# The written-out opening of a spectral mixer with a gated feed-forward: a new order, sixteen of its operations on GpSimd, and a root of its own for each of the first two blocks

## The chip, the core and the metric

The kernel runs on one core of a Trainium2 chip. The metric is device microseconds of one execution. The engines are named as the profile names them: PE is TensorE, whose weight loads stand apart as PEld; DVE is VectorE; ACT is ScalarE; POOL is GpSimd; SP is SyncE, which here only issues DMAs.

## The reference, cut to what matters

The input x is 1 x 2048 x 448 in fp32. It is normalised over its rows of 448, and the sum of three things is returned: x itself, a two-dimensional Fourier filter of the normalised x, and a gated feed-forward layer of it with 1792 inner columns.

```python
xn = layernorm(x)                                  # over the last axis, eps 1e-5
A = irfft2(rfft2(xn) * (w_r + 1j * w_i))           # 2048 x 448
gate, up = xn @ W_gate, xn @ W_up                  # 448 -> 1792
B = (gate * (gate > 0) * up) @ W_down              # 1792 -> 448
return x + A + B
```

## The kernel before

**Tiling.** The 2048 rows are 16 blocks of 128, number n2 = q + 4j, in four chunks q taken in the order 0, 2, 1, 3. The 1792 inner columns are 14 slabs f of 128, in groups of 5, 5 and 4. An fp32 operand is split into an fp16 upper part and an fp16 remainder, and a product is three fp16 passes. For slab f and chunk q, PE does 20 passes of 512 columns over gate (g = 0) and up (g = 1) into two PSUM banks (`gu_full`, L757) and a few "half" passes (`gu_half`, L764). ACT and DVE turn the banks into h (L799, L803, L807, L811), and `dn_mm` (L834) multiplies h by W_down. The Fourier part is cut into many DVE operations that run beside the feed-forward.

**What a block needs before PE can use it.** Statistics on DVE (`st`, L255 and L258), a reciprocal root on ACT (`sq`, L266) with three or four small corrections on DVE (`rs`, L271 to L275), the normalised fp32 block (`xn` on DVE at L297, or `ax` on ACT at L295), its upper half (`hi` or `hx`, ACT, L304 and L306), two small copies on POOL (`cp`, L310 and L311), and the remainder (`lo`, DVE, L321 and L322). For chunk 0, PE transposes the block (`tpA`, `tpB`, L337) and it is copied from PSUM into T (`vev` on DVE). The blocks of chunk 2 are transposed by DMA (`dm`, L330).

**What a weight needs.** A load (`lw`), the sum of its squares on ACT (`wsq`, L185), a sum over all partitions on POOL (`par`, `partition_all_reduce`, L188), two small scale operations on DVE (`wsc`, L191 and L195), its upper part on ACT (`whi`, L699) and its remainder on DVE (`wlo`, L703). For W_down the same steps are `lwd`, `wdq`, `wdp` (the all-reduce over `wdm`, L188), `wdsc` (ten small DVE operations), `wdh` (ACT, L731) and `wdl`.

**What sets the order.** In the opening, about the first 45 us, every engine's queue is in the order of a hand-written string of names, `OPENING`; each name issues one piece. Behind it, a scheduler puts units (`gu`, `dn`) and Fourier pieces into order. All queues are in order: an instruction that waits holds all that stand behind it on its engine. `keep_warm(n)` issues n matmuls on zeros (L1094), 21 of them at the start and 4 after the first transposes (`kw4`). Slab 0 is done in halves of 256 columns (`hh`, `lh`, `hl`), slab 1 too (`ah`, `bh`, `ch`), since two blocks of chunk 0 are ready before the other two.

**POOL before.** In the opening it does the memsets at the start, the small copies and the all-reduces, and nothing else.

Of the kernel before, what the change touches and what calls it, by code (L numbers as in the profile page):

```python
# [29 lines left out]
OPENING = """lx0 st0 lx4 st4 sqA rsA ax4 hi0 lx8 st8 lx12 xn0 lw cp0 lw lw lw hx4 warm tpA4 st12 tpA0 lo0 lx6 sqB rsB cp4 lo4  # L30
wsqW0g0 tpB0 kw4 tpB4 wsqW0g1 lx2 hi8 parW0g0 wscW0g0 lwd1 whiW0g0 vevA0 parW0g1 wscW0g1 vevA4 hh00 tpA8 whiW0g1
ly4 hi12 lw hh10 lw lw lw wsqW1g1 wsqW1g0 vevB4 vevB0 hl00 wloW0g0 parW1 wloW0g1 tpA12 vevA12 hl10 vevA8 lh00
cp8 xn8 lh10 hh11 lw ax12 lh11 wscW1 whiW1g0 hh01 cp12 whiW1g1 lh01 lw lo8 wsqW2g1 wsqW2g0 tpB8 ah00 lwd0 lo12
tpB12 wsqW3g0 vevB8 wloW1g0 ah10 wsqW3g1 vevB12 ah01 parW2 ah11 lwd2 wloW1g1 wscW2 bh00 hl11 hl01 lx14 whiW2g0
bh01 hp0 ch10 whiW2g1 lw st2 bh11 st6 re0 wloW2g0 bh10 wsqW4g1 ch00 ch11 tm0 gu2g0 parW3 wscW3 st14 wsqW4g0
whiW3g0 wloW2g1 ch01 ly0 parW4 wscW4 whiW3g1 wloW3g1 lw wsqW5g1 lx10 whiW4g0 wloW3g0 gh0 re1 st10 gu2g1 tm1 hp2
sqC rsC wsqW5g0 xn6 gu3g0 re2 parW5 wscW5 whiW5g0 tm2 wloW4g0 xn10 xn14 hx14 lwd4 hx6 lo6 hi10 whiW5g1 lo10
gu4g0 hx2 wloW5g0 whiW4g1 cp14 xn2 wdq0 gl0 cp10 gu3g1 wloW4g1 lo14 lwd3 wdq4 wdq2 cp2 re3 tm3 cp6 wloW5g1 gh1
gu4g1 gh2 wdq3 ly12 lo2 hp4 wdq1 wdp wdsc wdh4 dm10 gl1 re4 ly8 wdh3 gl2 gu5g1 tm4 gh4 dm14 gl4 dm6 gu5g0 dm2
re5 lfd gz0g0 wdl3 gz0g1 tm5 hp6 gh3 gl3 rz0 gh5 wdl4 gl5 wdh1 wdl1 wdh2 wdl2 n0 wdh0 wdl0 gz1g0 tz0 gz1g1 rz1  # L40
hz0 tz1 hz1 lz0 lz1
"""
EXPMASK = 0x7F800000
EXPONE = float(1 << 23)
# [100 lines left out]
def tile_gfnet_reglu(ctx: ExitStack, tc: tile.TileContext, x, xr, xi, wgu, wd, wf, c_fd, c_fm, c_im, c_row, c_id,  # L145
                     out):
    nc = tc.nc
    V, A, P, G = nc.vector, nc.scalar, nc.tensor, nc.gpsimd
# [28 lines left out]
    eps = mt([128, 1], F32, "eps")  # L177
# [23 lines left out]
    def ft(shape, dt, name, bufs=1):  # L201
        return fwd_pool.tile(shape, dt, name=name, bufs=bufs)
# [4 lines left out]
    warm = row_t.rearrange("p a b c -> p (a b c)")  # L207


    xr_t, xr_b = {}, {}  # L210
# [16 lines left out]
    wst, wdst, fm_t, im_t, wf_t = {}, {}, {}, {}, {}  # L227
# [22 lines left out]
    mv = {}  # L250

    def ln_stats(q, j):
        n2 = q + 4 * j
        st = ft([128, 6], F32, "bst", 2)
        V.bn_stats(st, xr_t[n2])  # L255
        if j == 0:
            mv[q] = ft([128, 4, 2], F32, "mv", 2)
        V.bn_aggr(mv[q][:, j, :], st)  # L258

    rst = {}  # L260

    def ln_sd(q, js=(0, 1, 2, 3)):
        w = ft([128, 4, 4], F32, "rs", 3)
        n = len(js)
        rst[q, js[0]] = w[:, :, 0:n], mv[q][:, js[0]:js[-1] + 1, :]
        A.activation(w[:, 0, 0:n], rst[q, js[0]][1][:, :, 1], AF.Abs_reciprocal_sqrt, bias=eps)  # L266

    def ln_rstd(q, js=(0, 1, 2, 3), bias=False):
        w, m = rst[q, js[0]]
        r0, t, r, nm = (w[:, i] for i in range(4))  # L270
        V.scalar_tensor_tensor(t, m[:, :, 1], 1e-5, r0, op0=OP.add, op1=OP.mult)  # L271
        V.scalar_tensor_tensor(t, t, -0.5 * 2048, r0, op0=OP.mult, op1=OP.mult)
        V.scalar_tensor_tensor(r, t, 1.5 * 2048, r0, op0=OP.add, op1=OP.mult)
        if bias:
            V.scalar_tensor_tensor(nm, m[:, :, 0], -1.0, r, op0=OP.mult, op1=OP.mult)  # L275
        for i, j in enumerate(js):
            rst[q, j] = r[:, i:i + 1], nm[:, i:i + 1], m[:, i, 0:1]

    xn, tt, xn_b = {}, {}, {}
    tts = [ft([128, 8, 128], F16, f"tt{i}") for i in range(4)]  # L280
# [6 lines left out]
        tt[n2] = tts[state.setdefault("tn", 0) % 4]  # L287
        state["tn"] += 1

    def ln_xn(n2, act=False):  # L290
        xn_b[n2] = free.pop(0)
        xn[n2] = xn_b[n2].rearrange("p g c k -> p (g c k)")[:, 0:D]
        r, nm, mean = rst[n2 % 4, n2 // 4]
        if act:
            A.activation(xn[n2], xr_t[n2], AF.Identity, scale=r, bias=nm)  # L295
        else:
            V.tensor_scalar(xn[n2], xr_t[n2], mean, r, op0=OP.subtract, op1=OP.mult)  # L297

    def ln_hi(n2, fused=False):
        new_tt(n2)  # L300
        o = tt[n2].rearrange("p a b -> p (a b)")[:, 0:D]
        r, nm, _ = rst[n2 % 4, n2 // 4]
        if fused:
            A.activation(o, xr_t[n2], AF.Identity, scale=r, bias=nm)  # L304
        else:
            A.activation(o, xn[n2], AF.Copy)  # L306
# [9 lines left out]
        ln_copy(n2)  # L316
        free.append(xr_b.pop(n2))

    def ln_lo(n2):
        x, t = xn[n2], tt[n2].rearrange("p a b -> p (a b)")  # L320
        V.tensor_tensor(t[:, 512:896], x[:, 0:384], t[:, 0:384], op=OP.subtract)  # L321
        V.tensor_tensor(t[:, 448:512], x[:, 384:448], t[:, 384:448], op=OP.subtract)  # L322
        free.append(xn_b.pop(n2))

    tp, last = {}, {}
# [350 lines left out]
    wt, wdt, wsc = {}, {}, {}  # L676
# [17 lines left out]
        for i, k in enumerate(gs):  # L694
            wsc[f, k] = sc[:, i:i + 1]

    def w_hi(f, g):
        w = wt[f, g] = mt([128, 8, 128], F16, "wt", 2 * NR + 4)
        A.activation(w[:, 0:4, :], wst[f, g], AF.Copy, scale=wsc[f, g])  # L699

    def w_lo(f, g):
        st, sc, w = wst[f, g], wsc.pop((f, g)), wt[f, g]
# [386 lines left out]
    seq1 = [(r + 4 * k, r) for k in (0, 1) for r in range(3)]  # L1089
    seq2 = [(r, r + 4) for r in range(3)] + [(3, 3)]  # L1090

    def keep_warm(n):
        for _ in range(n):
            P.matmul(wps, warm[:, 0:128], warm, start=True, stop=True)  # L1094

    pieces = {"lfd": lambda: nc.sync.dma_start(fd_t, c_fd),
              "lw": load_wn, "warm": lambda: keep_warm(NWARM),
              **{f"kw{n}": (lambda n=n: keep_warm(n)) for n in (1, 3, 4)},
              "wdp": lambda: wd_sum(len(groups[0])),
              "wdsc": lambda: wd_scale(0, groups[0])}  # L1100

    def piece(name, fn, *a):
        pieces[name] = lambda: fn(*a)

    for c, q in enumerate(CHUNKS[:2]):
        for js, tag in (((0, 1), "A"), ((2, 3), "B")) if c == 0 else (((0, 1, 2, 3), "C"),):
# [101 lines left out]
    for i, u in list(enumerate(units))[START + 1:-4]:  # L1208
        is_gu = u[0] == "gu"
        if is_gu:  # L1210
            _, g, f, q = u
# [4 lines left out]
        else:  # L1216
            _, g, n2, _ = u
# [69 lines left out]
```

## Time and profile before

| | us |
|---|---|
| median of 3 runs | 443.17 (442.64 to 443.61) |
| span of the profiled execution | 440.9 |
| PE busy | 435.7 (99% of the span) |
| DVE busy | 382.3 (87%) |
| ACT busy | 184.5 (42%) |
| POOL busy | 29.4 (7%) |

The span runs from the first to the last instruction of one profiled execution; the median of the runs is 2.27 us above it, which is what lies around the span. A row of the timeline gives the start, the time taken, the engine, the line, the operation, what it writes and reads, how many were merged, and in brackets the idle time before and what ended it. PEld shows when PE had to wait for weights: PE's own rows have modelled ends and hide small waits.

### The profile page before, as it was taken

The numbers are of one execution on the slowest core, as the hardware profiler recorded it, in microseconds if no ns is written. First come the engines' busy times: TensorE is split into PE (matmuls) and PEld (weight loads), VectorE is DVE, ScalarE is ACT, GpSimd is POOL, SyncE is SP. The second block draws the span as 40 slices with busy tenths as digits, with TensorE's granted clock in tenths as the row PEclk, the third lists the DMA queues.
The fourth block names the chain that finished last, engine by engine and source line by source line (L and its number), as shares of the span: only waits on it lengthen the run. The fifth ranks groups of instructions, "written<-read, shape, count | busy, mean of one in ns | idle before, by whom it ended". The sixth has DMA issues, their size and how long they took to land.

```text
span 440.9 us, 7429 instructions
## 1 busy us (share of the span) xinstructions
PE 435.7 (99%) x2641; PEld 221.9 (50%) x2641; DVE 382.3 (87%) x957; ACT 184.5 (42%) x396; POOL 29.4 (7%) x75
## 2 busy tenths in 40 slices
PE   8999999999999999999999999999999999999996
PEld 3744464554445545444545444444545555555664
DVE  6998496989887879999999999988997989798644
ACT  6995427392457236144023467233113332243220
POOL 3230002011100040000000020000000000000000
PEclk9999999999999999999999999999999999999999
DMA  7929895304111123332220210001111121210212
GB/s 256 301 91 198 269 364 172 70 2 107 59 49 50 47 76 119 94 118 84 86 84 1 84 43 1 0 1 42 44 43 49 54 91 34 72 55 33 89 51 104
DMA packets 37613, 39.55 MB, mean 90 GB/s; under 512 B 16535, under 2 KB 33353, under 8 KB 37577
## 3 DMA queue, kind: packets, MB, share of 16 engines
q1 hardware_dynamic: 37576, 39.09, 29.1%
q8 instruction: 20, 0.33, 0.3%
q14 instruction: 17, 0.13, 0.1%
HBM read 24.38 MB, written 3.67 MB: 64 GB/s over the span
## 4 chain that ended last, share of the span: by engine, by line
PE 90%; DVE 4%; ACT 3%; DMA 1%; issue 1%; SPq 0%; POOL 0%; ACTq 0%
PE bank L757 49%; PE bank L834 27%; PE bank L764 3%; PE fx L648 2%; PE fx L369 2%; PE fx L667 2%; PE fx L406 2%; PE bank L853 2%; ACT wt L699 1%; DMA T<-tt 1%; ACT junk L185 1%; DVE bst L255 1%; DVE wt L703 1%; DMA y<-in_xr 1%; ACT tt L304 1%
## 5 line engine op out<-in xcount | busy, mean ns | idle before, releaser
L757 PE MATMUL bank<-T,wt 128*128 128x512 f16 (+1 forms) x1160 | 252.7, 372 | 0.6 <-DVE T L345 0.5
L757 PEld LDWEIGHTS <-wt 128*128 128x128 f16 x1160 | 110.9, 98 | 127.6 <-issue 7.2
L834 PE MATMUL bank<-wdt,h 128*128 128x448 f16 x624 | 122.4, 352 | 0.0
L834 PEld LDWEIGHTS <-h 128*128 128x128 f16 x624 | 60.5, 98 | 55.1
L799 ACT ACTIVATE g<-bank 128x512 f32<-128x512 f32 x56 | 33.0, 591 | 80.4 <-PE bank L757 45.2
L807 ACT ACTIVATE h<-g 128x512 f16<-128x512 f32 x56 | 35.0, 627 | 70.1 <-DVE g L803 70.0
L803 DVE SCALAR_TENSOR_TENSOR g<-bank,g 128x512 f32<-128x512 f32 x56 | 38.2, 683 | 11.9 <-PE bank L757 6.8
L811 DVE TENSOR_TENSOR h<-g,h 128x512 f16<-128x512 f32 x56 | 38.1, 684 | 6.7 <-ACT h L807 6.4
L840 DVE SCALAR_TENSOR_TENSOR xy<-bank,dsc,xy 128x448 f32<-128x448 f32 x44 | 29.8, 676 | 5.5 <-PE bank L834 5.2
L632 ACT ACTIVATE vt<-y,fsc 128x456 f16<-128x456 f32 x15 | 10.1, 674 | 34.5 <-issue 14.0
L699 ACT ACTIVATE wt<-wst,wsc 128x512 f16<-128x512 f32 x28 | 19.3, 713 | 11.1 <-DVE wsc L195 10.3
L703 DVE SCALAR_TENSOR_TENSOR wt<-wst,wsc,wt 128x512 f16<-128x512 f32 x28 | 20.4, 742 | 0.5 <-ACT wt L699 0.3
L672 DVE SCALAR_TENSOR_TENSOR xy<-fx,fsc,xy 128x448 f32<-128x448 f32 x16 | 10.8, 680 | 10.9 <-PE fx L667 10.9
L188 POOL PARTITION_ALL_REDUCE wm<-wm x15 | 10.5, 697 | 139.9 <-ACT junk L185 136.4
L185 ACT ACTIVATE junk<-wst 128x512 bf16<-128x512 f32 x28 | 17.2, 616 | 0.0
L397 ACT ACTIVATE Xh<-X 128x456 f16<-128x456 f32 x16 | 9.3, 579 | 16.4 <-DVE X L395 9.3
L764 PE MATMUL bank<-T,wt 64*128 64x512 f16 x112 | 15.6, 380 | 0.0
L400 DVE TENSOR_TENSOR Xh<-X,Xh 128x456 f16<-128x456 f32 x16 | 9.8, 624 | 4.9 <-ACT Xh L397 4.9
L648 PE MATMUL fx<-im,vt 128*128 128x128 f16 x192 | 13.3, 219 | 0.0
L667 PEld LDWEIGHTS <-pgh 114*128 114x128 f16 x192 | 10.9, 98 | 3.8 <-issue 0.8
L648 PEld LDWEIGHTS <-vt 128*128 128x128 f16 x192 | 11.6, 98 | 1.3
L406 PE MATMUL fx<-Xh,fm 128*128 128x456 f16 x48 | 12.2, 356 | 0.0
(168 smaller groups left out, 480.1 us busy)
## 6 DMA issues: line engine op xcount, KB each, us to landing
wst<-in_wgu SPq DMA_DIRECT2D x28, 256.0 KB
sw<-y SPq DMA_DIRECT2D x56, 112.2 KB
wf<-in_wf SPq DMA_DIRECT2D x16, 228.0 KB
xy<-in_x SPq DMA_DIRECT2D x16, 224.0 KB
y<-in_xr SPq DMA_DIRECT2D x15, 224.0 KB
out<-xy SPq DMA_DIRECT2D x15, 224.0 KB
wdst<-in_wd SPq DMA_DIRECT2D x14, 224.0 KB
fm<-in_c_fm SPq DMA_DIRECT2D x4, 256.0 KB
```

The source lines that it names most:

```text
L185: A.activation(mt([128, 512], BF16, "junk", 2)[:, 0:src.shape[-1]], src, AF.Square, scale=SQ, accum_out=acc)
L648: P.matmul(o, v[:, h, w], m[:, c, :], start=(i == 0), stop=(i == 2), skip_group_check=True)
L699: A.activation(w[:, 0:4, :], wst[f, g], AF.Copy, scale=wsc[f, g])
L703: V.scalar_tensor_tensor(w[:, 4:8, :], st, sc, w[:, 0:4, :], op0=OP.mult, op1=OP.subtract)
L757: last["P"] = P.matmul(hps[f, q][g][:, cs], wt[f, g][:, a, :], Tq[q][:, b, cs], start=(start and i == 0), stop=(stop and i == len(seq) - 1 ...
L764: m = P.matmul(hps[f, q][g][:, 0:512], wt[f, g][rows, 7, :], Tq[q][rows, b, :], start=start, stop=stop).ins
L799: last["A"] = A.activation(g1s[f, q], hps[f, q][0], AF.Relu, scale=2.0 ** -22).ins
L803: last["V"] = V.scalar_tensor_tensor(g1, hps[f, q][1], 2.0 ** -22, g1, op0=OP.mult, op1=OP.mult).ins
L807: A.activation(ht[f, q][:, 0, :], g1s[f, q], AF.Copy)
L811: V.tensor_tensor(h[:, 1, :], g1s.pop((f, q)), h[:, 0, :], op=OP.subtract)
L834: last["P"] = P.matmul(ps[:, 0:D], ht[f, q][:, a, js], wdt[f][:, b, :], start=(i == 0), stop=(i == n - 1)).ins
L840: last["V"] = V.scalar_tensor_tensor(xy[:, n2, :], dps[n2][:, 0:D], dsc[:, g:g + 1], xy[:, n2, :], op0=OP.mult, op1=OP.add).ins
```

## The change

`OPENING` is replaced by another string of the same work. What differs beyond the order:

- Sixteen pieces go to POOL. Four `px` (blocks 4, 14, 6 and 10) and four `ph` (8, 6, 10, 2) are a `tensor_scalar` over 448 columns, the normalised block or its upper half straight from x. Four `pl` (4, 8, 14, 2) are the two `tensor_tensor` of the remainder. Four `pw` (W0g1, W2g0, W2g1, W4g0) are a `tensor_scalar` over 512 columns, the upper part of a weight.
- Blocks 4 and 0 each get their own root (`sq4 rs4`, `sq0 rs0`), where before one root served both (`sqA rsA`). Block 4 is loaded ahead of block 0.
- Blocks 0 and 4 are multiplied with slab 0 in quarters of 128 columns (`hq`, `lq`, `kq`); the other two blocks stay one half of 256.
- 14 warm matmuls stand at the start in place of 21; five of the eight copies from PSUM into T go from DVE to ACT (`aev`).

The scheduler's part behind the opening comes out in another order on every engine, with the same operations.

```diff
-NWARM = 21
-OPENING = """lx0 st0 lx4 st4 sqA rsA ax4 hi0 lx8 st8 lx12 xn0 lw cp0 lw lw lw hx4 warm tpA4 st12 tpA0 lo0 ...
+OPENING = """lx4 lx0 lw st4 sq4 st0 rs4 wsqW0g0 parW0g0 lw lx8 sq0 rs0 px4 lx12 warm14 wscW0g0 wsqW0g1 xn0 hx4 st8 tpA4 parW0g1 pl4
+hx0 cp0 st12 cp4 whiW0g0 wscW0g1 lw lo0 wloW0g0 lw tpA0 kw4 sqB vevA4 tpB0 aevA0 hq00 tpB4 ...
-    def ln_xn(n2, act=False):
+    def ln_xn(n2, act=False, pool=False):
...
-            V.tensor_scalar(xn[n2], xr_t[n2], mean, r, op0=OP.subtract, op1=OP.mult)
+            (G if pool else V).tensor_scalar(xn[n2], xr_t[n2], mean, r, op0=OP.subtract, op1=OP.mult)
-    def ln_hi(n2, fused=False):
+    def ln_hi(n2, fused=False, eng=None):
...
+        if eng is not None:
+            eng.tensor_scalar(o, xr_t[n2], mean, r, op0=OP.subtract, op1=OP.mult)
-    def ln_lo(n2):
+    def ln_lo(n2, eng=V):
...
-        V.tensor_tensor(t[:, 512:896], x[:, 0:384], t[:, 0:384], op=OP.subtract)
-        V.tensor_tensor(t[:, 448:512], x[:, 384:448], t[:, 384:448], op=OP.subtract)
+        eng.tensor_tensor(t[:, 512:896], x[:, 0:384], t[:, 0:384], op=OP.subtract)
+        eng.tensor_tensor(t[:, 448:512], x[:, 384:448], t[:, 384:448], op=OP.subtract)
-    def w_hi(f, g):
+    def w_hi(f, g, eng=None):
...
+            eng.tensor_scalar(w[:, 0:4, :], wst[f, g], wsc[f, g], None, op0=OP.mult)
...
+            piece(f"sq{n2}", ln_sd, q, (j,))
+            piece(f"rs{n2}", ln_rstd, q, (j,))
+            piece(f"nm{n2}", ln_bias, q, (j,))
+                                ("px", ln_xn, False, True), ("ph", ln_hi, False, G), ("pl", ln_lo, G), ("vh", ln_hi, False, V), ("dm", ln_dma),
+            piece(f"pwW{f}g{g}", w_hi, f, g, G)
```

POOL's queue at the start of the opening, before. `wm` is the buffer of the weights' sums, `tt` a transposed-to-be block, `Tl` a buffer that is cleared. An `ISA` row with names is an all-reduce; the one without names is added by the build, and it is the only one of its kind behind the start of the program.

```order
L284 MEMSET Tl_98 32x512
L310 COPY tt_100<-tt_100 128x48
L311 COPY tt_100<-tt_100 128x64
L310 COPY tt_101<-tt_101 128x48
L311 COPY tt_101<-tt_101 128x64
L188 ISA
L188 ISA wm<-wm 128x1 x2
L188 ISA wm<-wm 128x2
```

The same place now (`y_68` is the normalised block 4, `g_122` its input, `wt` a weight's two parts):

```order
L287 MEMSET Tl_98 32x512
L187 ISA
L187 ISA wm<-wm 128x1
L300 ISA
L300 TENSOR_SCALAR y_68<-g_122,mv,rs 128x448
L187 ISA
L187 ISA wm<-wm 128x1
L326 ISA
L326 TENSOR_TENSOR tt_100<-y_68,tt_100 128x384
L327 TENSOR_TENSOR tt_100<-y_68,tt_100 128x64
L315 COPY tt_101<-tt_101 128x48
L316 COPY tt_101<-tt_101 128x64
```

The nameless row stands wherever the queue goes from an all-reduce to a `TENSOR_SCALAR` or `TENSOR_TENSOR` or back, and never between an all-reduce and a `COPY`. There was one in the whole kernel; there are 13 now, all in the opening, the last of them ahead of the all-reduce over `wdm`.

POOL's queue at the end of the opening, before: the last small copies of the opening, then the all-reduce of W_down's sums.

```order
L310 COPY tt_103<-tt_103 128x48
L311 COPY tt_103<-tt_103 128x64
L310 COPY tt_101<-tt_101 128x48
L311 COPY tt_101<-tt_101 128x64
L188 ISA wdm<-wdm 128x5
```

And now, behind the twelfth nameless row:

```order
L307 ISA
L307 TENSOR_SCALAR tt_102<-y_75,mv,rs 128x448
L707 TENSOR_SCALAR wt<-wst,wsc 128x512
L307 TENSOR_SCALAR tt_103<-y_72,mv,rs 128x448
L326 TENSOR_TENSOR tt_103<-y_79,tt_103 128x384
...
L300 TENSOR_SCALAR y_80<-y_75,mv,rs 128x448
L326 TENSOR_TENSOR tt_101<-y_77,tt_101 128x384
L327 TENSOR_TENSOR tt_101<-y_77,tt_101 128x64
L315 COPY tt_102<-tt_102 128x48
L316 COPY tt_102<-tt_102 128x64
L187 ISA
L187 ISA wdm<-wdm 128x5
```

The upper part of W4g0 (the `wt` row) and the all-reduce over `wdm` moved behind all of POOL's new work; ahead of `dn_mm`, PE needs both.

ACT's queue at the start, before (`rs` is a root, `junk,wm` a sum of squares, `tt<-y` an upper half):

```order
L266 ACTIVATE rs<-mv,eps 128x2
L295 ACTIVATE y_67<-g_127,rs 128x448
L304 ACTIVATE tt_100<-y_66,rs 128x448
L306 ACTIVATE tt_101<-y_67 128x448
L266 ACTIVATE rs<-mv,eps 128x2
L185 ACTIVATE junk,wm<-wst 128x512 x2
```

And now:

```order
L265 ACTIVATE rs<-mv,eps 128x1
L184 ACTIVATE junk,wm<-wst 128x512
L265 ACTIVATE rs<-mv,eps 128x1
L184 ACTIVATE junk,wm<-wst 128x512
L311 ACTIVATE tt_100<-y_68 128x448
L311 ACTIVATE tt_101<-y_70 128x448
L705 ACTIVATE wt<-wst,wsc 128x512
```

ACT no longer makes the normalised block 4 itself; its upper half `tt_100<-y_68` now waits for POOL, and the other upper half and the first weight stand behind that wait.

More of the change, by code (lines that the diff above doesn't have):

```diff
@@ L25 @@
 LAG, AHEAD, RAMP = 1, 5, 8
-NWARM = 21
 N2ORD = [0, 8, 4, 12, 2, 10, 6, 14, 1, 9, 5, 13, 3, 11, 7, 15]
 CHUNKS = [0, 2, 1, 3]
[L30 to L38, printed above, removed]
@@ L42 @@
+gh1 gu3g0 wloW4g0 ph2 tm2 wloW5g1 pl2 wloW5g0 cp2 lo6 gu3g1 cp6 wloW4g1 gu4g0 px10 wdq2 re3 tm3 gu4g1 ly12 gh2 gl2
+lo10 pl14 hp4 cp10 wdq4 dm2 gu5g1 wdq1 gh3 wdp gu5g0 dm10 ly0 wdsc wdh4 cp14 dm6 wdh0 gl1 re4 re5 tm4 gl3 tm5 wdh3
+wdh1 dm14 gz0g0 gh4 wdl4 gl4 ly8 gh5 wdl1 gz0g1 hp6 rz0 gz1g0 gl5 tz0 gz1g1 hz0 rz1 wdl0 wdh2 wdl3 lz0 tz1 hz1 wdl2
+lz1
 """
@@ L255, in ln_stats @@
         V.bn_stats(st, xr_t[n2])
-        if j == 0:
+        if q not in mv:
             mv[q] = ft([128, 4, 2], F32, "mv", 2)
         V.bn_aggr(mv[q][:, j, :], st)
-    rst = {}
+    rst, rsb = {}, {}
     def ln_sd(q, js=(0, 1, 2, 3)):
-        w = ft([128, 4, 4], F32, "rs", 3)
+        w = ft([128, 4, 4], F32, "rs", 4)
         n = len(js)
-        rst[q, js[0]] = w[:, :, 0:n], mv[q][:, js[0]:js[-1] + 1, :]
-        A.activation(w[:, 0, 0:n], rst[q, js[0]][1][:, :, 1], AF.Abs_reciprocal_sqrt, bias=eps)
+        rsb[q, js[0]] = w[:, :, 0:n], mv[q][:, js[0]:js[-1] + 1, :]
+        A.activation(w[:, 0, 0:n], rsb[q, js[0]][1][:, :, 1], AF.Abs_reciprocal_sqrt, bias=eps)
     def ln_rstd(q, js=(0, 1, 2, 3), bias=False):
-        w, m = rst[q, js[0]]
+        w, m = rsb[q, js[0]]
         r0, t, r, nm = (w[:, i] for i in range(4))
@@ L274, in ln_rstd, with ln_bias @@
         if bias:
-            V.scalar_tensor_tensor(nm, m[:, :, 0], -1.0, r, op0=OP.mult, op1=OP.mult)
+            ln_bias(q, js)
         for i, j in enumerate(js):
             rst[q, j] = r[:, i:i + 1], nm[:, i:i + 1], m[:, i, 0:1]
+    def ln_bias(q, js):
+        w, m = rsb[q, js[0]]
+        V.scalar_tensor_tensor(w[:, 3], m[:, :, 0], -1.0, w[:, 2], op0=OP.mult, op1=OP.mult)
     xn, tt, xn_b = {}, {}, {}
@@ L695, in w_scale @@
             wsc[f, k] = sc[:, i:i + 1]
-    def w_hi(f, g):
+    def w_hi(f, g, eng=None):
         w = wt[f, g] = mt([128, 8, 128], F16, "wt", 2 * NR + 4)
-        A.activation(w[:, 0:4, :], wst[f, g], AF.Copy, scale=wsc[f, g])
+        if eng is None:
+            A.activation(w[:, 0:4, :], wst[f, g], AF.Copy, scale=wsc[f, g])
+        else:
+            eng.tensor_scalar(w[:, 0:4, :], wst[f, g], wsc[f, g], None, op0=OP.mult)
     def w_lo(f, g):
@@ L1096, in tile_gfnet_reglu @@
     pieces = {"lfd": lambda: nc.sync.dma_start(fd_t, c_fd),
-              "lw": load_wn, "warm": lambda: keep_warm(NWARM),
-              **{f"kw{n}": (lambda n=n: keep_warm(n)) for n in (1, 3, 4)},
+              "lw": load_wn, **{f"{t}{n}": (lambda n=n: keep_warm(n)) for t in ("kw", "warm") for n in range(1, 25)},
               "wdp": lambda: wd_sum(len(groups[0])),
@@ L1151, in tile_gfnet_reglu @@
             piece(f"whiW{f}g{g}", w_hi, f, g)
+            piece(f"pwW{f}g{g}", w_hi, f, g, G)
+            piece(f"vwW{f}g{g}", w_hi, f, g, V)
             piece(f"wloW{f}g{g}", w_lo, f, g)
@@ L1154, in tile_gfnet_reglu @@
             if f == 0:
+                for j in range(2):
+                    for tag, sq in (("hq", seq1[0:3]), ("lq", seq1[3:6]), ("kq", seq2)):
+                        piece(f"{tag}{g}{j}", gu_full, f, q, (g,), slice(128 * j, 128 * j + 128), tag == "hq" and j == 0,
+                              False, sq)
                 piece(f"parW{f}g{g}", w_sum, f, (g,))
```

16 lines of the change are left out of this document (10 added, 6 removed).

## The prediction

> **What bounds the kernel now.** I read the page's busy times first, then PE's timeline, then the waits of its weight loads, then POOL's timeline. The columns of a timeline row are start, time taken, engine, line, operation and, in brackets, the idle time before it and what ended it.
>
> ```profile
> PE 435.7 (99%) x2641; PEld 221.9 (50%) x2641; DVE 382.3 (87%) x957; ACT 184.5 (42%) x396; POOL 29.4 (7%) x75
> 1.22 7.46 PE L1094 MATMUL bank<-row_t 128*128 128x512 f16 x21 [1.22 <-DVE row_t L1166]
> 8.52 0.78 PE L337 MATMUL fx<-g,tt 128*128 128x128 f16 x11
> 9.13 1.03 PE L1094 MATMUL bank<-row_t 128*128 128x512 f16 x4
> 10.93 0.49 PE L757 MATMUL bank<-T,wt 128*128 128x256 f16 x3 [0.49 <-DVE T L345]
> 35.73 9.09 PE L757 MATMUL bank<-T,wt 128*128 128x512 f16 x40
> 33.09 1.63 PEld L757 LDWEIGHTS <-wt 128*128 128x128 f16 x9 [0.32 <-DVE wt L703]
> 35.19 0.12 PEld L764 LDWEIGHTS <-wt 64*128 64x128 f16 x4 [0.47 <-DVE wt L703]
> 40.33 0.76 PEld L757 LDWEIGHTS <-wt 128*128 128x128 f16 x5 [0.60 <-DMA T<-tt]
> ```
>
> PE bounds the kernel, and its work is the same before and after. Time can only be won where PE does nothing useful: before 8.52 (warm matmuls), up to the first pass of slab 0 at 10.93, and in waits of 0.3 to 0.6 us. An opening without any fault would win some 3 us. It can lose without limit: whatever PE waits for in the opening moves all that follows.
>
> **What POOL does now, and the price of its new work.** In the opening POOL waits more than it works:
>
> ```profile
> 1.03 1.44 POOL L284 MEMSET Tl<- 32x512 f16 x3
> 7.58 0.22 POOL L310 COPY tt<-tt 128x48 f16<-128x48 f16 x1 [5.11 <-ACT tt L304]
> 8.93 0.39 POOL L188 PARTITION_ALL_REDUCE wm<-wm  x1 [0.28 <-ACT junk L185]
> 31.77 0.68 POOL L310 COPY tt<-tt 128x48 f16<-128x48 f16 x1
> L188 POOL PARTITION_ALL_REDUCE wm<-wm x15: 392/423/2199, 8.9 to 260.4; - x15
> L188 POOLq MODIFY_POOL_CONFIG  x2: 5/5/5, 8.7 to 8.7; - x2
> L311 POOL COPY tt<-tt 128x64 f16<-128x64 f16 x8 | 3.2, 401 | 0.0
> L297 DVE TENSOR_SCALAR y<-y,mv,rs 128x448 f32<-128x448 f32 x6 | 2.9, 504 | 0.0
> L321 DVE TENSOR_TENSOR tt<-y,tt 128x384 f16<-128x384 f32 x8 | 4.6, 569 | 0.0
> L322 DVE TENSOR_TENSOR tt<-y,tt 128x64 f16<-128x64 f32 x8 | 1.8, 222 | 0.0
> ```
>
> The two rows of L188 in the middle come from the view of one line (count, then least, median and largest ns): 15 all-reduces, and two MODIFY_POOL_CONFIG records at 8.7. These two are the nameless ISA row of the built program; they stand just ahead of the first all-reduce, at 8.93. The changed kernel has 13 such rows. So a pair of records changes what POOL is set up to run, all-reduces and copies on one side, TENSOR_SCALAR and TENSOR_TENSOR on the other. The whole prediction hangs on what one change costs; call it c.
>
> What the trace shows of c is one pair, behind which POOL is idle for 0.28 us until ACT releases the all-reduce. That is the lower bound. But it is a special pair: this program never sets POOL up for anything else, so if the set-up outlasts an execution, which no row shows, the pair asks for what is there already and need not have fetched anything. The Trainium skill, "GPSIMD Engine Reference", section 2.1 (Instruction dispatch), says that the first call into freshly loaded code pays about 6 us (5.95 measured) that no instruction of the profile shows; the pair at 8.7 disagrees, unless nothing was loaded there; by that figure the sum below would give 507.3.
>
> For a pair that goes to the other set and back, the nearest rows are a fetch from memory, and an engine that takes in a table:
>
> ```profile
> 0.73 1.28 ACT L1165 ACT_TABLE_LOAD   x1 [0.73 <-PEq L1275]
> 0.74 0.39 SPq L225 DMA_DIRECT2D y<-in_xr  x1
> 3.31 0.63 DVE L255 BATCH_NORM_STATS2 bst<-y 128x6 f32<-128x448 f32 x1 [2.14 <-DMA y<-in_xr]
> 5.00:10.00 5.00, 5.00 (x29) 2.44 (x28) 4.45 (x19) 4.16 (x10) 1.87 (x6) 1.00 0.95 309
> ```
>
> From issue at 0.74 to first use at 3.31, a fetch takes 2.57 us on empty queues. I take c = 6.42 us as an estimate: one fetch for each of the two records (5.14) and one table load (1.28). Lower, without the table load, 5.14. Upper, with two 256 KB loads ahead in the queue at the 309 GB/s that the last row shows for 5 to 10 us, 1.66 more: 8.1. A single fetch, 2.57, and the 0.28 of the row are rivals below. I choose the fetch over the 0.28 because the code for the other set has to come from somewhere and no row shows POOL keeping two.
>
> The arithmetic: POOL's memset of 512 columns takes 1.44 / 3 = 0.48, so 448 columns can't be much under 0.42; DVE takes 0.50, 0.57 and 0.22. A copy of 48 columns takes 0.22 when DVE is quiet and 0.68 at 31.77, when DVE is busy. I take 0.8 for a TENSOR_SCALAR of 448, 0.9 for one of 512 and 1.2 for a remainder (two TENSOR_TENSOR), some 1.5 times DVE's; bounds half and double that. The Trainium skill, "SBUF — State Buffer", section "Who interferes with whom", says that a DVE instruction with two SBUF inputs and a GpSimd one that reads SBUF lock each other out; the 0.22 and 0.68 agree.
>
> **The sum.** With c of several us, POOL never waits again: its queue is the path. Up to the all-reduce over wdm it holds:
>
> - start at 1.03 + 1.44 = 2.47;
> - 13 changes, 13c;
> - 7 all-reduces of 0.423 for the weights and one of 0.44 for wdm: 3.4;
> - 8 TENSOR_SCALAR of 448 (6.4), 4 of 512 (3.6), 4 remainders (4.8): 14.8;
> - 14 copies at 0.23 (0.40 where DVE is busy): 3.3.
>
> That ends at 24.0 + 13c. Then come W_down's scales on DVE and two upper parts on ACT, and `dn_mm` may start:
>
> ```profile
> 36.00 0.44 POOL L188 PARTITION_ALL_REDUCE wdm<-wdm  x1 [2.87 <-ACT junk L185]
> 36.48 0.17 DVE L191 TENSOR_SCALAR ed<-wdm 128x5 uint32<-128x5 uint32 x1 [0.74 <-POOL wdm L188]
> 38.01 0.23 DVE L727 TENSOR_SCALAR wds<-wds 128x5 f32<-128x5 f32 x1
> L731 ACT ACTIVATE wdt<-wdst,wds 128x448 f16<-128x448 f32 x5 | 3.1, 658 | 2.4 <-DVE wds L727 2.4
> ```
>
> From 36.44 to 38.24 it is 1.8, and 2 x 0.66 = 1.3: the first `dn_mm` at 27.1 + 13c. In the changed order it stands right behind slab 5; before, what stands behind slab 5 is the second 20 of the 40 passes at 35.73, whose weights are loaded at 40.33. So the end moves by 27.1 + 13c − 40.3 = 13c − 13.2. With c = 6.42 that is 70.3. PE is 99% busy from there on and can't win it back, and the DVE work of the Fourier part stands behind the opening in the same queues. Span 440.9 + 70.3 = 511.2; with the 2.27 by which the median of the runs stands above the span, **513.5 us**. With c = 5.14 it is 496.8, with 8.1 it is 535.3. Half or double the arithmetic would move this by −7.4 or +14.8, which the same range mostly holds.
>
> Slab 4, earlier in the queue, agrees: its upper part `wt` stands behind 12 changes, 7 all-reduces (3.0), 6 + 4 TENSOR_SCALAR (8.4), 2 remainders (2.4) and 8 copies (1.9), at 18.2 + 12c = 95.2, while PE's weights for its second half were there at 33.09. Over 60 us are lost by then; wdm adds the rest.
>
> **The other parts.** Warm matmuls: 14 instead of 21 cost nothing, since PE then waits for block 4 in any case. PE goes cold while it waits: the first row, 7.46 us for 21 passes, is 0.36 each where 40 passes take 9.09, 0.22 each. That slow restart lies beside POOL's queue, which sets the date of `dn_mm`; without that cover it costs up to 2.9 us (21 x 0.14) once. Quarter passes: the same columns, in 40 passes for 20; 11 passes of 128 take 0.78 and 40 of 512 take 9.09, 0.07 against 0.22, so at most 20 x 0.02 = 0.4 us. The separate roots and the five copies that go to ACT lie on engines that would wait for POOL. The new order of the loads and the chunk-2 DMA transposes wait for POOL's copies too and come early enough for their users. The scheduler's order behind the opening I put at nothing: PE idles 5.2 us in the whole span, so it can win at most that; bounds ±1.5, from the waits of 0.3 to 0.6 in the rows above.
>
> **The rivals.**
>
> *A change costs what the row shows, 0.28 us.* For it: the only pair in the trace. Against it: that pair changed nothing. Then 13 x 0.28 = 3.6 us fit into POOL's waits (5.11 before 7.58), and block 4 comes a little earlier: statistics at 3.31 to 4.15 instead of second, root and corrections to about 5.5, all-reduce and change to 6.0, POOL's 0.8 to 6.8, ACT's upper half to 7.4 instead of 7.9. The first pass moves from 10.93 to some 10.4, later waits come and go: 442.6, between 441 and 444. This is the case that is not slower. It decides below c of about 1, where 13c − 13.2 turns negative. Chance 0.13.
>
> *Changes are cheap but POOL's arithmetic isn't.* For it: copies at 0.68 for 0.22 beside a busy DVE. With c = 0.28 and arithmetic and copies at twice my price (36.2 instead of 18.1), `dn_mm` starts at 27.1 + 3.6 + 18.1 = 48.8, 8.5 late; POOL's waits on ACT add nothing while it is behind: 451.7. Chance 0.06.
>
> *One fetch for a change.* c = 2.57: 13 x 2.57 − 13.2 = 20.2, so 463.4. For it: two records may need only one load. Against: nothing in the trace tells. Chance 0.09.
>
> *The forecast*, c from 5 to 8 and a little beyond: 0.72, of which some 0.06 lies above 536.
>
> **How the numbers follow.** The time is that of the likeliest case, 513.5, whose own range is 497 to 536. The range for 8 in 10 has to reach into the rivals: from 443 to 536 it leaves out the part of the first rival below 443 (0.09) and the forecast's upper end (0.06). Faster by over 0.2% (0.9 us, about what a measurement of this kernel can tell from no change) is half of the first rival, 0.06; within 0.2% 0.06; slower 0.88.
>
> **What would show it.** In the changed profile: MODIFY_POOL_CONFIG 26 times in the opening; POOL's TENSOR_SCALAR of block 4 near 16 us instead of 6; POOL idle for several us ahead of each change with nothing to release it; PE with idle stretches of 5 to 13 us between 7 and 110 us; and the first `dn_mm` near 110 us. It is wrong if POOL's first TENSOR_SCALAR starts less than 1 us behind the all-reduce ahead of it, if PE's first pass of slab 0 is before 12 us, or if the lost time lies behind the opening.

## The result and the profile after

The changed kernel takes 534.54 us (median of 5 runs, 533.37 to 535.9), against 443.17 before: a ratio of 1.206, 95% interval 1.204 to 1.208. The profiled execution spans 532.7 us. The prediction said 513.5 and 443 to 536.

The busy times and the row of PE's clock, from the page of the changed kernel:

```profile
PE 451.8 (85%) x2654; PEld 227.3 (43%) x2654; DVE 381.1 (72%) x945; ACT 181.1 (34%) x393; POOL 55.6 (10%) x95
PEclk8555877577999999999999999999999999999999
```

PE went from 99% busy to 85%, and the slices of the clock row (13.3 us each) show at most eight tenths up to about 130 us: PE often stands still and often runs at a lower granted clock. POOL worked for only 26 us more than before. Its timeline shows where the time is:

```profile
6.33 0.39 POOL L187 PARTITION_ALL_REDUCE wm<-wm  x1 [3.86 <-ACT rs L265]
16.11 1.88 POOL L300 TENSOR_SCALAR y<-g,mv,rs 128x448 f32<-128x448 f32 x1 [9.40 <-DMA wst<-in_wgu]
24.02 0.40 POOL L187 PARTITION_ALL_REDUCE wm<-wm  x1 [6.03 <-issue]
31.36 0.90 POOL L326 TENSOR_TENSOR tt<-y,tt 128x384 f16<-128x384 f32 x1 [6.94 <-issue]
32.24 0.30 POOL L327 TENSOR_TENSOR tt<-y,tt 128x64 f16<-128x64 f32 x1
33.22 1.57 POOL L707 TENSOR_SCALAR wt<-wst,wsc 128x512 f16<-128x512 f32 x1
41.39 0.41 POOL L187 PARTITION_ALL_REDUCE wm<-wm  x1 [6.60 <-issue]
49.02 1.88 POOL L307 TENSOR_SCALAR tt<-y,mv,rs 128x448 f16<-128x448 f32 x1 [7.23 <-issue]
...
95.11 0.41 POOL L187 PARTITION_ALL_REDUCE wm<-wm  x1 [5.96 <-issue]
103.04 1.88 POOL L307 TENSOR_SCALAR tt<-y,mv,rs 128x448 f16<-128x448 f32 x1 [7.52 <-issue]
121.58 0.46 POOL L187 PARTITION_ALL_REDUCE wdm<-wdm  x1 [5.96 <-DMA T<-tt]
L187 POOLq MODIFY_POOL_CONFIG  x14: 1/1/12, 2.5 to 115.8; - x14
```

The last row is from the view of one line: seven of the 13 pairs lead to an all-reduce; the other six stand at the lines of the arithmetic. Each pair but the first has a silence of 5.8 to 9.4 us behind it. The sign to look for is `issue` in the brackets: nothing that the profile shows was being waited for. At 16.11 the brackets name a DMA, yet all that this TENSOR_SCALAR reads was there at 5.42, when DVE's last correction ended. The first pair, at 2.5, was free, as before: the all-reduce at 6.33 had waited for ACT's sum, whose last operation ended at 6.15.

PE's timeline, at the places where it waited, and behind the opening:

```profile
18.66 0.97 PE L342 MATMUL fx<-g,tt 128*128 128x128 f16 x6 [11.43 <-ACT tt L311]
106.54 0.61 PE L765 MATMUL bank<-T,wt 128*128 128x512 f16 x1 [19.07 <-POOL wt L707]
114.97 4.49 PE L765 MATMUL bank<-T,wt 128*128 128x512 f16 x20
125.14 0.90 PE L842 MATMUL bank<-wdt,h 128*128 128x448 f16 x2 [5.68 <-ACT wdt L739]
125.83 6.45 PE L765 MATMUL bank<-T,wt 128*128 128x512 f16 x20
170.62 6.16 PE L765 MATMUL bank<-T,wt 128*128 128x512 f16 x20 [3.25 <-DMA T<-tt]
```

PE waits for what POOL makes or for what stands behind POOL's queue: block 4's upper half at 18.66, W4g0 at 106.54, W_down at 125.14. The last two rows are new: 20 passes that took 4.49 at 114.97 take 6.45 and 6.16 behind a wait, because the granted clock is 0.50 for 3.4 to 4 us of them (called half clock below).

### The profile page after: what moved, and what is told of

The parts are those of the page before. It is cut to its first block, busy times and chain, and to the rows that moved or that the text cites. A ratio compares the mean times of both kernels' runs of the same rounds, so it can differ in the third digit from the quotient of the medians.

```text
span 532.7 us, 7478 instructions
## 1 busy us (share of the span) xinstructions
PE 451.8 (85%) x2654; PEld 227.3 (43%) x2654; DVE 381.1 (72%) x945; ACT 181.1 (34%) x393; POOL 55.6 (10%) x95
## 4 chain that ended last, share of the span: by engine, by line
PE 70%; issue 9%; DMA 7%; POOL 6%; DVE 4%; SPq 2%; ACT 2%; POOLq 0%; ACTq 0%; DVEq 0%
PE bank L765 39%; PE bank L842 20%; PE bank L772 2%; PE fx L653 2%; DMA y<-in_xr 2%; DMA wst<-in_wgu 2%; PE fx L672 2%; PE bank L861 2%; POOL tt L307 1%; POOL y L300 1%; PE fx L411 1%; PE fx L374 1%; DMA T<-tt 1%; DMA fm<-in_c_fm 1%; POOL wt L707 1%
## 5 line engine op out<-in xcount | busy, mean ns | idle before, releaser
L765 PE MATMUL bank<-T,wt 128*128 128x512 f16 (+2 forms) x1180 | 266.2, 383 | 30.7 <-POOL wt L707 25.6
L765 PEld LDWEIGHTS <-wt 128*128 128x128 f16 x1180 | 116.3, 102 | 166.7 <-POOL wt L707 26.4
L807 ACT ACTIVATE g<-bank 128x512 f32<-128x512 f32 x56 | 33.1, 592 | 96.8 <-PE bank L765 51.7
L711 DVE SCALAR_TENSOR_TENSOR wt<-wst,wsc,wt 128x512 f16<-128x512 f32 x28 | 22.5, 814 | 18.1 <-POOL wt L707 17.1
L190 DVE TENSOR_SCALAR eg<-wm 128x2 uint32<-128x2 uint32 (+1 forms) x15 | 2.7, 180 | 43.9 <-POOL wm L187 43.9
L705 ACT ACTIVATE wt<-wst,wsc 128x512 f16<-128x512 f32 x24 | 16.6, 713 | 44.8 <-DVE wsc L194 42.4
L342 PE MATMUL fx<-g,tt 128*128 128x128 f16 x24 | 3.6, 289 | 22.4 <-ACT tt L311 11.4
L342 PEld LDWEIGHTS <-tt 128*128 128x128 f16 x32 | 2.7, 122 | 38.1 <-POOL tt L307 13.5
L653 PE MATMUL fx<-im,vt 128*128 128x128 f16 x192 | 13.3, 219 | 0.0
L739 ACT ACTIVATE wdt<-wdst,wds 128x448 f16<-128x448 f32 x14 | 8.9, 660 | 12.3 <-DVE wds L735 10.9
```

Source lines behind the costliest of these rows:

```text
L653: P.matmul(o, v[:, h, w], m[:, c, :], start=(i == 0), stop=(i == 2), skip_group_check=True)
L711: V.scalar_tensor_tensor(w[:, 4:8, :], st, sc, w[:, 0:4, :], op0=OP.mult, op1=OP.subtract)
L765: last["P"] = P.matmul(hps[f, q][g][:, cs], wt[f, g][:, a, :], Tq[q][:, b, cs], start=(start and i == 0), stop=(stop and i == len(seq) - 1 ...
L807: last["A"] = A.activation(g1s[f, q], hps[f, q][0], AF.Relu, scale=2.0 ** -22).ins
```

## The experiments

The theory: each change of POOL's set-up holds its in-order queue for some 6 to 7 us, the arithmetic adds to it, and PE waits for the queue's end. The rivals: slow arithmetic and its conflicts with DVE; the order, roots and loads by themselves; a change that costs one fetch or nothing. Before was run beside each of them, at 442.8 to 443.0.

**The changes without the arithmetic.** The sixteen pieces went back to DVE and ACT, and a tiny addition took each one's place:

```diff
-... rs0 px4 lx12 ...
+... rs0 xn4 dp lx12 ...
+"dp": lambda: G.tensor_tensor(state["dmy"][:, 1:2], state["dmy"][:, 0:1], state["dmy"][:, 0:1], op=OP.add)
```

> As the kernel without GpSimd's arithmetic, but at each of the sixteen places GpSimd adds two numbers per partition in a scratch buffer that nobody reads, so that the 13 changes of set-up stay and the arithmetic goes. Theory (12 paid changes of about 6.8 us hold GpSimd's queue, and the all-reduces behind them hold PE): the 27.2 us of arithmetic become about 1.6, so 534.5 - 25.6 = 509, between 500 and 517. Rival (slow arithmetic and its port conflicts with DVE carry most of the loss): below 465.

It took 509.45 us (508.89 to 510.18). POOL's timeline:

```profile
6.74 0.39 POOL L187 PARTITION_ALL_REDUCE wm<-wm  x1 [4.10 <-ACT junk L184]
15.97 0.18 POOL L1108 TENSOR_TENSOR dmy<-dmy 128x1 f32<-128x1 f32 x1 [8.85 <-issue]
22.21 0.40 POOL L187 PARTITION_ALL_REDUCE wm<-wm  x1 [6.05 <-issue]
29.58 0.18 POOL L1108 TENSOR_TENSOR dmy<-dmy 128x1 f32<-128x1 f32 x1 [6.97 <-issue]
36.46 0.41 POOL L187 PARTITION_ALL_REDUCE wm<-wm  x1 [5.85 <-issue]
```

An addition of one column, on data that has long been there, needs 7 to 9 us to start. The arithmetic was worth 534.54 − 509.45 = 25.1 us of 25.6 expected, and the rival that it carries most of the loss falls.

**The arithmetic without the changes.** In the opening, `all_sum` only copies:

```diff
-        G.partition_all_reduce(o, i, 128, bass_isa.ReduceOp.add)
+        if "opened" in state:
+            G.partition_all_reduce(o, i, 128, bass_isa.ReduceOp.add)
+        else:
+            G.tensor_copy(o, i)
```

> The changed kernel with all of GpSimd's arithmetic, but in the opening each all-reduce is a GpSimd copy of the same one or more columns, so that the sums of squares stay those of one partition each (the sum over the partitions is left out, the weights' scales are not the reference's). The set-up then changes twice in place of 13 times, once at the start and once behind the opening. Theory (changes cost 6.8 us each, the arithmetic 27.2 in all): GpSimd's queue ends at 2.5 + 9.4 + 27.2 + 5 = 44 and the first dn_mm stands at 47, 7 later than before: 450, between 444 and 458. Rival (the arithmetic and its conflicts carry the loss): over 490.

It took 466.53 us (466.18 to 468.53): 68 less than the changed kernel, but outside the range. POOL's timeline:

```profile
6.25 0.19 POOL L190 COPY wm<-wm 128x1 f32<-128x1 f32 x1 [3.78 <-ACT junk L184]
14.19 1.88 POOL L303 TENSOR_SCALAR y<-g,mv,rs 128x448 f32<-128x448 f32 x1 [7.75 <-DMA wst<-in_wgu]
51.55 0.18 POOL L190 COPY wdm<-wdm 128x5 f32<-128x5 f32 x1
```

I had the one paid change begin at 2.5; it begins behind the first copy, at 6.4, and POOL also waits some 4 us in between for ACT and DVE, so the queue ends at 51.7 instead of 44. The rest is in part what the next kernel shows; behind waits of 2.73 and 3.00 us for `T<-tt` PE also ran 20 passes in 6.16.

**No arithmetic on POOL at all.** `px` and `pl` go to DVE, `ph` and `pw` to ACT, everywhere in the new order:

```diff
-... rs0 px4 lx12 ... pl4 ... pwW0g1 ... ph8 ...
+... rs0 xn4 lx12 ... lo4 ... whiW0g1 ... hi8 ...
```

> The changed kernel with its new order, own roots, quarters and ACT evictions, but the sixteen pieces back on DVE (px, pl) and ACT (ph, pw). Theory (GpSimd's changes of set-up and its arithmetic are the whole loss): 440 to 446, within 3 us of before, and one pair of MODIFY_POOL_CONFIG in place of 13. Rival (the order, the roots or the order of the loads lose by themselves): over 450, with PE idle for more than 5 us in the opening.

It took 451.84 us (451.25 to 454.39; ratio 1.020 to 1.024). One row of POOL's records, from the view of a line, and two of PE's timeline:

```profile
L186 POOLq MODIFY_POOL_CONFIG  x2: 1/1/1, 2.5 to 2.5; - x2
```

```profile
47.52 4.48 PE L764 MATMUL bank<-T,wt 128*128 128x512 f16 x20 [1.29 <-DMA T<-tt]
90.47 6.16 PE L764 MATMUL bank<-T,wt 128*128 128x512 f16 x20 [3.39 <-DMA T<-tt]
```

The changes are gone, and PE still comes late: chunk 2, which started at 40.33 before, starts at 47.52, and at 90 stand the wait and the slow passes that the changed kernel has at 170. My theory that POOL is the whole loss falls: 9 us stay without it. In this execution, whose span is 11.6 us longer than before's, 7.2 lie ahead of chunk 2 and 4.4 behind its start, where the wait at 90 and its half clock take 5.1.

**The same, all on DVE.**

```diff
-... lo4 ... whiW0g1 ... hi8 ...
+... lo4 ... vwW0g1 ... vh8 ...
```

> The changed kernel with all sixteen pieces on DVE, in place of DVE and ACT. In the kernel without GpSimd's arithmetic ACT was busy for 5.00 of 5 us at 15 to 20 and at 25 to 35, and PE idle 8 us before the second group. Theory (that ACT load made its 9 us over before, not the order, roots or loads): 8 upper parts of about 0.7 us leave ACT, and the time falls to 444 to 448. Rival (the new order itself loses): 451 or more.

It took 450.33 us (448.31 to 452.99; ratio 1.013 to 1.018): by the medians ACT's load was some 1.5 of the 9, though the ranges of the two kernels overlap, and the rival is nearer than the theory. PE's timeline:

```profile
8.82 0.97 PE L341 MATMUL fx<-g,tt 128*128 128x128 f16 x6 [2.22 <-ACT tt L310]
9.58 1.91 PE L1101 MATMUL bank<-row_t 128*128 128x512 f16 x4
12.61 0.33 PE L764 MATMUL bank<-T,wt 128*128 128x128 f16 x3 [0.58 <-ACT T L347]
86.92 6.16 PE L764 MATMUL bank<-T,wt 128*128 128x512 f16 x20 [2.31 <-DMA T<-tt]
```

Slab 0 starts at 12.61 instead of 10.93, and the wait for `T<-tt` stands at 87, with the half clock behind it. SP's timeline at that place, before and in this kernel:

```profile
71.27 1.68 SPq L558 DMA_DIRECT2D row<-y  x2
73.13 5.51 SPq L330 DMA_TRANSPOSE T<-tt  x4
```

```profile
77.76 2.69 SPq L334 DMA_TRANSPOSE T<-tt  x2
80.56 1.69 SPq L562 DMA_DIRECT2D row<-y  x2
82.42 2.88 SPq L334 DMA_TRANSPOSE T<-tt  x2
```

Two small DMAs have come between the transposes of chunk 1. That suggested the next kernel.

**The transposes together.**

```diff
-            last["R"] = nc.sync.dma_start(row[j + 8 * par:j + 8 * par + 1], cur["s1", j, par][64:65]).ins
+            with tc.high_priority(offset=-3000):
+                last["R"] = nc.sync.dma_start(row[j + 8 * par:j + 8 * par + 1], cur["s1", j, par][64:65]).ins
```

> The kernel with all sixteen pieces on DVE, and behind the opening the DMAs that write row put off, so that on SP no row DMA stands between the four DMA transposes of chunk 1 any more (one load still does). Theory (in every kernel with the new order PE waits 2.3 to 3.4 us for T<-tt there and then runs 20 passes at half clock, 6.16 in place of 4.49, because two row DMAs stand between the transposes; before they stood ahead of them): 4 us less, 446, between 444.5 and 448. Rival (the transposes are late because their blocks are, or those us come back elsewhere): 449 or more.

It took 452.43 us (451.77 to 454.49), so nothing was won. SP's timeline, and from the kernel before PE's first pass of chunk 1, which had no wait:

```profile
79.57 2.70 SPq L334 DMA_TRANSPOSE T<-tt  x2
82.39 0.52 SPq L223 DMA_DIRECT2D y<-in_xr  x1
83.08 3.35 SPq L334 DMA_TRANSPOSE T<-tt  x2
```

```profile
80.25 1.02 PE L757 MATMUL bank<-T,wt 128*128 128x512 f16 x4
```

From the first transpose to PE's pass it is 88.17 − 79.57 = 8.60 us instead of 86.92 − 77.76 = 9.16; before, it was 80.25 − 73.13 = 7.12. The row DMAs were worth some 0.6 us of that. That the transposes are late because their blocks are, the rival's first half, does not fit the rows; that those us come back elsewhere, its second half, does. SP does wait 7.5 us for a block's remainder ahead of the first transpose, but counted from PE's start of chunk 2 this one is no later than before: 79.57 − 46.85 = 32.72 us, against 73.13 − 40.33 = 32.80. What is longer is the time that the four take in SP's queue: 6.86 us here and 7.54 with the row DMAs, against 5.51 before. The load of x still stands between them here; whether the wait would go with that load put off as well was not tried.

At this place the clock stayed up (20 passes in 4.48), but in this execution PE waited 3.5 us for a load of x at the start, where the other had 2.22 for ACT, and 2.3 for DVE's `g`, where the other had 1.6: what was won at chunk 1 is not in the time. With 20 warm matmuls as well:

```diff
-... xn4 lx12 warm14 ...
+... xn4 lx12 warm20 ...
```

> The same with 20 warm matmuls at the start in place of 14. Theory (with 14 PE idles 2.2 us before its first transposes and runs at half clock until 15 us, which GpSimd's queue covers in the changed kernel and nothing covers here): 1 to 2 us less than with 14. Rival (slab 0 waits for its weights and blocks, not for PE): no difference beyond 0.5.

451.87 us (450.8 to 453.5), within the spread of the one with 14, although the granted clock was 1.00 from 0 to 19 us, where the one with 14 had 0.50 from 12 to 18. Here the rival holds. At chunk 1 the half clock was back: 20 passes in 6.16 behind a wait of 1.96 us.

**Fewer warm matmuls, this part alone,** in the kernel before:

```diff
-NWARM = 21
+NWARM = 14
```

> The kernel before with 14 warm matmuls at the start in place of 21, this part of the change alone. Theory (PE then idles some 2.5 us before 8.5 and its clock is halved for what follows): 1 to 3 us slower, 444 to 446. Rival (PE waits for blocks and weights there in any case): 442.8 plus or minus 0.9.

442.64 us (ratio 0.998 to 1.000): no difference, and the rival holds. PE's timeline:

```profile
8.29 0.94 PE L337 MATMUL fx<-g,tt 128*128 128x128 f16 x11 [2.56 <-ACT tt L306]
9.07 1.03 PE L1094 MATMUL bank<-row_t 128*128 128x512 f16 x4
```

After 2.56 us of idling four warm matmuls took 1.03, as before; in the kernel on DVE four took 1.91 after 2.22 us.

**One trip to the other set and back.** The kernel before with a single tiny addition (`dp`, as above), between the first two all-reduces (early) or behind the one over `wdm` (late):

```diff
-... hi8 parW0g0 wscW0g0 ...
+... hi8 parW0g0 dp wscW0g0 ...
```

```diff
-... wdq1 wdp wdsc ...
+... wdq1 wdp dp wdsc ...
```

> The kernel before, with one GpSimd addition of one column (nobody reads it) between the all-reduces over the sums of W0g0 and W0g1, so with one change to the arithmetic set and one back, while the loads of the opening run. Theory (a change holds GpSimd's queue 6.9 to 9.4 us on the way there and about 6 back): the all-reduce that was at 9.54 comes at 23 to 26, PE waits for W0g1 nearly as long, and the time is 443 + 13 = 456, between 452 and 461. Rival (one fetch of 2.57 for a change): 447. Rival (a change costs what the row of before shows, 0.28): 443.5.

> The kernel before, with one GpSimd addition of one column (nobody reads it) right behind the all-reduce over wdm, so with one change to the arithmetic set and one back, in a stretch in which GpSimd has nothing to do until about 60 us. Theory (a change holds GpSimd's queue alone, 7 us and 6): all of it is covered, 443.2 plus or minus 0.9. Rival (a change also holds DMA queues or other engines): 448 or more.

Early: 459.76 us (458.64 to 460.76). Late: 443.5 (442.89 to 443.99; ratio 1.0005 to 1.0023). POOL's timeline, early and then late:

```profile
9.06 0.39 POOL L187 PARTITION_ALL_REDUCE wm<-wm  x1 [0.34 <-ACT junk L184]
18.23 0.18 POOL L1100 TENSOR_TENSOR dmy<-dmy 128x1 f32<-128x1 f32 x1 [8.78 <-issue]
24.32 0.40 POOL L187 PARTITION_ALL_REDUCE wm<-wm  x1 [5.90 <-issue]
```

```profile
35.89 0.45 POOL L187 PARTITION_ALL_REDUCE wdm<-wdm  x1 [2.87 <-ACT junk L184]
43.26 0.18 POOL L1100 TENSOR_TENSOR dmy<-dmy 128x1 f32<-128x1 f32 x1 [6.92 <-issue]
70.59 0.22 POOL L309 COPY tt<-tt 128x48 f16<-128x48 f16 x1 [27.15 <-ACT tt L305]
```

Early, 14.7 us of silence cost 17 us, since an all-reduce stands behind them; late, the whole trip cost 0.7, since POOL has nothing to do until 70, and the way back, whose records stand at 74.0, lies within a wait for ACT that lasts until 91.76. The rivals of one fetch (447) and of 0.28 (443.5) fall with the early one.

**The other set left behind at the end.**

```diff
         all_sum(small[:, 17:18], small[:, 16:17])
+        G.tensor_tensor(small[:, 40:41], small[:, 17:18], small[:, 17:18], op=OP.add)
```

> The kernel before, with one GpSimd addition of one column (nobody reads it) behind its very last all-reduce, at some 260 us, where GpSimd has nothing more to do. An execution then ends with the arithmetic set in place. Theory (what was set up outlasts an execution, and the pair at 8.7 of before cost nothing because the all-reduce set was there already): the first all-reduce of the next execution, at 8.93 before, now waits 6 to 9 us behind that pair, and the time is 449 to 453. Rival (every execution starts from the same set-up, or the first pair is free for another reason): 442.8 plus or minus 0.9, with the first all-reduce near 8.9.

451.17 us (450.55 to 451.7; ratio 1.017 to 1.020). POOL's timeline at the start:

```profile
8.19 0.65 POOL L311 COPY tt<-tt 128x64 f16<-128x64 f16 x1
16.34 0.78 POOL L188 PARTITION_ALL_REDUCE wm<-wm  x2 [7.50 <-issue]
```

The pair that cost nothing before now costs 7.50 us, though all that was added stands at an execution's end: the set-up outlasts it.

**PE kept warm ahead of `dn_mm`,** in the changed kernel:

```diff
-... wdp gu5g0 dm10 ...
+... wdp gu5g0 warm24 dm10 ...
```

> The changed kernel with 24 more matmuls on zeros on PE between slab 5 and the first dn_mm, where PE waited 5.7 us for W_down. Theory (of the 7 us that the changed kernel loses behind its first dn_mm some 2 are PE's half clock after that wait: 20 passes in 6.45 us in place of 4.49): 532.5, between 531 and 533.5, and the 20 passes behind the first dn_mm in 4.5. Rival (those passes are slow because 327 GB/s of loads start there, or for another reason): 534.5.

530.37 us (529.36 to 531.34), 4.2 less where I had expected 2, and below my range. PE's timeline:

```profile
117.97 5.34 PE L1101 MATMUL bank<-row_t 128*128 128x512 f16 x24
124.44 4.48 PE L764 MATMUL bank<-T,wt 128*128 128x512 f16 x20
167.21 4.48 PE L764 MATMUL bank<-T,wt 128*128 128x512 f16 x20 [3.21 <-DMA T<-tt]
```

The passes behind `dn_mm` are back at 4.48, which is the 2. The wait at 167 is still there, but this time no half clock followed it, which is another 1.7. In this execution the first `dn_mm` also came 1.2 us earlier, at 123.95, with POOL's twelve silences 1.0 us shorter in sum; nothing in the edit asks for that.

**A copy on POOL,** in the kernel before:

```diff
-... xn14 hx14 lwd4 ...
+... xn14 hi14 lwd4 ...
-            A.activation(o, xn[n2], AF.Copy)
+            (G.tensor_copy(o, xn[n2]) if n2 in (10, 14) else A.activation(o, xn[n2], AF.Copy))
```

> The kernel before with the upper halves of blocks 14 and 10 as plain GpSimd copies (fp32 to fp16, 448 columns, from the normalised block) in place of two ACT operations. Theory (only TENSOR_SCALAR and TENSOR_TENSOR need the other set; a copy runs beside the all-reduces): still one pair of MODIFY_POOL_CONFIG, the copies below 2 us each, 442.8 plus or minus 1. Rival (a cast of a wide tile needs a change as well): GpSimd silent for 6 to 9 us ahead of the first copy and of the all-reduce over wdm, and 446 or more.

445.15 us (444.36 to 445.44; ratio 1.003 to 1.006). POOL's timeline:

```profile
29.59 1.39 POOL L305 CAST tt<-y 128x448 f16<-128x448 f32 x2 [2.81 <-DVE y L296]
```

No change of set-up, 0.70 us a copy, and the wait ahead of it is for DVE. It is slower by 2.2 all the same, beyond my range: among PE's waits stand two of 0.8 us, for `T<-tt` and for a weight's remainder, that are not among those of before.

## Why the prediction held, and where it did not

**The range.** The time lies inside it, but only 1.5 us below its end, and that is partly luck: the upper end was made for a larger c (8.1), and c was nearly right. What filled the range were the arithmetic, POOL's waits and the time behind `dn_mm`.

**c and the count.** Right in sum, by two errors, which is luck. The sum had 13 c with c = 6.42, 83.5. It was 12 paid changes: six to the arithmetic (9.40, 6.94, 7.23, 6.93, 6.87, 7.52, together 44.9) and six back (6.03, 6.60, 5.92, 5.83, 5.96, 5.96, together 36.3): 81.2, 6.77 each. The first pair is free, as the prediction allowed of such a pair, and the kernel that left the other set behind shows why.

The working of c (two fetches and a table) is borne out by nothing: the pages of before and after count the same 37 packets on the two queues of instructions, and those of the other kernels 36 to 38, whatever their number of changes. In the first 20 us of an execution the first paid change took longer (7.75 to 9.4 towards the arithmetic, 7.50 towards the all-reduce) than changes did later (6.8 to 7.5 and 5.7 to 6.6). DMAs moved 207 to 384 GB/s beside those first changes, but the late trip's 6.92 stood beside 251, so neither that loads lengthen a change nor that a change reads memory is shown.

The Trainium skill, "GPSIMD Engine Reference", section 2.1 (Instruction dispatch), gives 5.95 us for the first call into freshly loaded code. The way to the all-reduce agrees (5.74 to 6.60, but 7.50 in the kernel with the addition at its end); the way to the arithmetic took a microsecond longer. The prediction put copies on the side of the all-reduces; they run on both, since in the changed kernel they start at 32.49, right behind the TENSOR_TENSOR at 32.24, with no silence.

**The steps of the loss.** From 442.77, the new order without arithmetic on POOL adds 9.1, the changes with it 57.6 and the arithmetic 25.1. Taken the other way, the arithmetic adds 14.7 to the new order (with one change still paid) and the other changes 68.0. By either way the changes are the main part.

**The arithmetic.** This term was mis-sized. It had 14.8 and was 27.3: 1.87 for a TENSOR_SCALAR of 448 (priced 0.8), 1.57 for one of 512 (0.9), and 1.2 to 2.1 for a remainder (1.2). I had scaled from POOL's memset and from DVE; POOL's TENSOR_SCALAR is 3.7 times DVE's 0.50. Worth 12.5. The cross-check by slab 4 had the same prices, so it could not catch them: it gave 95.2, and W4g0's upper part ended at 106.5. Nor was DVE quiet beside the copy of 0.22 at 7.58: it ran a BATCH_NORM_STATS2, with one input; beside the 0.68 it ran a TENSOR_TENSOR with two.

**"POOL never waits again".** It waited 3.86 us for ACT's first sum and 0.79 for a correction: 4.65. In all 12.5 + 4.65 − 2.3 = 14.9; the all-reduce over `wdm` ended at 122.0 instead of 107.5, 14.5 late. From there to `dn_mm` it took 3.1, as predicted.

**"PE can't win it back, and the order behind the opening costs nothing, ±1.5".** The first half held; the second was too low by 7.0 us: from `dn_mm` to the end it took 407.6 instead of 400.6. It is 2.0 for the passes at 125.83, 3.25 for the wait on `T<-tt` and 1.7 for the passes behind it. The row DMAs between the chunk-1 transposes, part of what that wait comes from, could have been read from SP's queue. 14.5 + 7.0 is the whole difference of 21.5 between 511.2 and 532.7.

**The parts put at nothing.** The warm matmuls are: 14 for 21 makes no difference even without POOL's cover. The order, roots and quarters are not: with no arithmetic on POOL they are 7.5 to 9 us slower than before. A part of it is the wait for chunk 1 with its half clock: it stands in every kernel with the new order, with and without arithmetic on POOL, takes 1.8 to 5.1 us there, and is not in the kernel before. How much of the rest is the order itself and how much is work on DVE and ACT that the order meant for POOL stays open; of its places only the warm matmuls and the row DMAs were tried.

**The signs.** The 26 records and the silent changes were as told. Block 4 at 16.11 was too, but by luck: the first pair was free, POOL waited 3.86 us for ACT, and the change took 9.40. PE's waits were longer, up to 19.07, and `dn_mm` stood at 125 instead of 110. Of the signs of being wrong one came true in a small part: 7.0 of the 91 us lost lie behind the opening.

**The rivals.** A change for 0.28 and a change for one fetch fell with the early trip. Cheap changes with slow arithmetic would have been nearly right about the arithmetic (twice its price is 29.6, measured 27.3) and wrong about the time.

## What to carry to other kernels

Before giving an engine some more work, look in its queue for what it must exchange to do it: on GpSimd here, arithmetic among all-reduces costs about 13 us for each trip there and back, and the busy column shows none of it. Such a price belongs to the change and not to the work: one trip in a gap cost 0.7 us, the same trip ahead of a needed result 17, and the two copies, which need no exchange, took POOL only 0.70 us each, though that kernel was 2.2 us slower. A price read from the one row that a trace offers is worthless if that row was the free case, so ask what state it began in.

## What the runs showed of the hardware

- POOL's set-up is kept from one execution to the next: one instruction at an execution's end made the next one 8.4 us slower.
- In the three kernels with twelve paid changes, the way to the arithmetic took about a microsecond longer than the way to the all-reduce (6.83 to 7.52 against 5.74 to 6.60). A first way to the arithmetic within the first 20 us of an execution took 7.75 to 9.44; why is open.
- Whether a short wait costs PE its clock is not a matter of its length alone: waits of 1.96, 2.22, 2.31, 2.73, 3.00, 3.25 and 3.39 us were followed by half clock, waits of 1.75, 2.56 and 3.21 were not. Half clock can also come late: in the kernel with the transposes together a wait of 3.48 us ended at 9.51, and the granted clock stayed at 1.00 to 11 us and was 0.50 from 12 to 18. Executions of one kernel differ as well: with all sixteen pieces on DVE the mean granted clock was 0.992 in three and 0.999 in the fourth, the fastest (448.31 us). The Trainium skill, "TensorE: Matmul & The Clock Gate", section "What's actually happening", has the clock halved after an idle window of about 3.4 us that runs freely; no run here shows that window. Half clock behind waits of 1.96 to 2.73 us does not fit a window that must be idle from end to end; short waits that go either way agree with one that is not tied to the kernel.
